# Pooled keys in pieces of 64, 16 and 64, and early sums and masks on TensorE, in a pooled and local attention with a feed-forward part

## The chip, the cores and the metric

The kernel runs on one core of a Trainium2 chip. The core has a matrix engine (TensorE, in the profile PE, with its weight loads as PEld), a vector engine (VectorE, DVE), a scalar engine (ScalarE, ACT), GpSimd (POOL), and SyncE (SP), which here only issues DMA transfers. TensorE reads SBUF, the working memory of 128 partitions, and writes PSUM, eight banks of 512 f32 values per partition. The metric is the device time of one execution in microseconds; it is a median over several runs.

## The reference

Inputs q, k and v are 8 batches x 8 heads x 576 tokens x 64 values. For each head two attentions are added. The result of all heads of a token, 512 values, goes through a feed-forward part with a softmax-weighted activation and a layer norm.

```python
# factor 4: means over four neighbouring tokens, 144 pooled tokens
q_d = q.reshape(B, H, Sd, 4, D).mean(axis=3)      # k_d, v_d the same way
out_d = sm_attn(q_d, k_d, v_d)                    # softmax(q k^T / 8) v
out_up = np.repeat(out_d, 4, axis=2)
# local: token i sees tokens j with |i - j| < 4
mask = np.abs(pos[:, None] - pos[None, :]) < 4
out_local = softmax(np.where(mask, scale * q @ k^T, -1e9)) @ v
x = (out_up + out_local) as 4608 tokens x 512
# feed-forward
h = x @ w_in                                      # 512 -> 1024, weights given as float64
solu = h * softmax(h)
ln = (solu - mean) / sqrt(var + 1e-6) * g_ln
return ln @ w_out                                 # 1024 -> 512
```

## The kernel before

**Steps and their order.** The kernel writes its work as a list of numbered steps (`plan`), and the string `ORDER` at its head gives the order in which they are issued: 2099 numbers before. Nothing reorders them afterwards; each engine, and SyncE's DMA queue, takes its instructions in that order and waits where one needs another engine. Steps 0 to 23 are `keep_clock`, pairs of matmuls on zeros that keep TensorE busy. The last loop of the function runs the plan.

**A batch.** For the first two batches (`EarlyBatch`) q and k of a head pair are loaded with six tokens per partition, turned by ordinary f32 matmuls with an identity (tiles `qp` and `kp`, L478) and copied to `qT` and `kT` (L484). For the other six, `Batch.pair_steps` loads 32x32 blocks and turns them on VectorE (L411, L415). In all eight, `sums` (L367) adds four neighbouring tokens of `qT` and `kT` on VectorE into `qd_flat` and `kd`; the division by 4 is left to a scale in the softmax.

**Local attention** (`Local.by_tensor`, five units a batch, each with two windows of 64 tokens for all heads): scores `sc` on TensorE (L614); on VectorE the mask is added while the scores leave PSUM (L632), and the maximum taken (L637); GpSimd subtracts it (L639); ScalarE takes the exponential (L641); VectorE sums (L644); GpSimd multiplies by the reciprocal (L650); TensorE turns the result (`plt`, L660), ScalarE copies it (L663), TensorE multiplies by v (`xp`, L670). A branch for a mask by TensorE is there (`early`), but `MASKED = 0` leaves it unused.

**Pooled attention** (`Pooled.steps`, one unit per head pair): the 144 pooled queries are taken in three chunks of 48 (`QC`, `QN`). Scores `sd` (L696) lie with 64 rows of one chunk and head in each half of the partitions. After the softmax (L703 to L720) `pdt` (L731) turns the weights with 12 transposes into two pieces of 72 keys on 72 partitions; two copies (L738, L741 or L743) bring them to `pdT`; `po` (L752) multiplies by the pooled v, `vd`, for two key pieces and two heads. `load_vs` loads v for the pooled sums in four transfers a batch, of 72 partitions each; GpSimd adds (L434, L437).

**Where matmuls sit in the array.** A matmul with at most 64 rows of input (partitions) and 64 columns of weights takes a quarter of the 128x128 array; the quarter follows from the partitions of its input and its output. `sc`, `xp` and `sd` are of this kind. `pdt` uses halves by rows, `po`, `qp` and `kp` halves by columns, and `plt` and the feed-forward matmuls the whole array.

**Weights and feed-forward.** w_in and w_out come as float64 in 16 pieces. ScalarE and VectorE make f32 of the two halves of each number (L323 to L338); ScalarE rounds to fp32r (L360), GpSimd takes the rest (L362), so that three products of rounded parts give the precision. For w_out, ScalarE first multiplies by `g_ln` (L358). A feed-forward tile has 128 tokens: `xhl` splits x (L919, L922), `ffn_in` makes h with 24 matmuls (L770) and the activation, `ffn_back` and `ffn_ut` bring it back turned through DRAM and VectorE (L866, L872, L874), `ffn_out` makes 24 matmuls (L888) and writes the output.

Of the kernel before, what the change touches and what calls it, by code (L numbers as in the profile page):

```python
# [129 lines left out]
def pooled_local_attention_then_solu_ffn(  # L130
# [701 lines left out]


    away = {}
    ON_PE = (NTILE - 1,)

    LATE = range(29, NTILE - 1)

# [203 lines left out]
```

## Time and profile before

| what | before |
|---|---|
| median of 3 runs | 601.65 us (601.19 to 605.02) |
| the profiled execution | 602.74 us, its span 601.0 us |
| granted TensorE clock, mean | 0.989 |
| busy: TensorE, VectorE, ScalarE, GpSimd | 574.8, 396.5, 361.8, 375.6 us |
| DMA | 94.34 MB, mean 157 GB/s |

The span reaches from the first to the last instruction of the program that was profiled; the execution's own time is 1.7 us longer. A line L752 is line 752 of the kernel. An f32 matmul shows as two records in the profile, a transpose as one. In rows of the timeline a block's length includes the time that its last matmul needs to run through the array, while the next block has begun already; so blocks are compared by the distance of their starts.

### The profile page before, as it was taken

What the parts mean: (1) busy time and instruction counts of PE and PEld (TensorE: products, weight loads), DVE (VectorE), ACT (ScalarE), POOL (GpSimd) and SP (SyncE); (2) the same over time, 40 slices, a digit from 0 to 9 for tenths busy, and PEclk for the clock granted to TensorE, in tenths of its full rate; (3) what the DMA queues carried; (4) which work ended last, traced back from release to release, by engine and by line L of the source; (5) the groups of instructions that cost most, each with busy time, mean ns of one, the idle gap of its engine ahead of it and who ended that gap; (6) DMA issues with size and microseconds to landing.
All of it is one profiled execution on the core that took longest, in us unless ns stands there. A gap on an engine that the chain in (4) does not pass through costs nothing.

```text
span 601.0 us, 15341 instructions
## 1 busy us (share of the span) xinstructions
PE 574.8 (96%) x5912; PEld 447.1 (74%) x5912; DVE 396.5 (66%) x692; ACT 361.8 (60%) x800; POOL 375.6 (62%) x553
## 2 busy tenths in 40 slices
PE   6889789899999999999999999999999999999996
PEld 3666557677777777787877777777777878788785
DVE  5989999869747677766856767737655533643541
ACT  3758866577745566566664854657465655553443
POOL 2576668867784778678574777656786767332221
PEclk8979999899999999999999999999999999999999
DMA  8999776687769767766878567847416623124230
GB/s 231 238 251 254 140 183 146 164 178 162 195 144 189 171 167 186 170 148 175 190 151 201 143 173 182 185 114 195 97 59 188 146 89 114 63 88 151 96 123 35
DMA packets 203913, 94.34 MB, mean 157 GB/s; under 512 B 162496, under 2 KB 192704, under 8 KB 203840
## 3 DMA queue, kind: packets, MB, share of 16 engines
q1 hardware_dynamic: 203840, 93.37, 63.3%
q8 instruction: 46, 0.75, 0.6%
q14 instruction: 27, 0.22, 0.1%
HBM read 65.54 MB, written 27.79 MB: 155 GB/s over the span
## 4 chain that ended last, share of the span: by engine, by line
PE 75%; POOL 6%; DVE 5%; ACT 4%; SPq 4%; DMA 3%; issue 3%; POOLq 0%; DVEq 0%
PE o L888 31%; PE h L770 27%; PE xp L670 3%; PE plt L660 3%; PE po L752 3%; PE sc L614 2%; DMA qm<-in_q_dram 2%; SPq L245 2%; PE pdt L731 2%; PE sd L696 2%; POOL pl L639 2%; DMA v<-u 1%; SPq L264 1%; POOL pd L720 1%; DVE w L334 1%
## 5 line engine op out<-in xcount | busy, mean ns | idle before, releaser
L888 PE MATMUL o<-wo_h,uh 128*128 128x512 f32 x288 | 117.9, 409 | 0.8 <-ACT uh L872 0.7
L770 PE MATMUL h<-wi_h,xh 128*128 128x512 f32 x288 | 116.3, 404 | 0.6 <-DVE e L785 0.6
L770 PE MATMUL h<-wi_h,xl 128*128 128x512 f32 x288 | 114.3, 397 | 1.3 <-POOL xl L922 1.3
L888 PE MATMUL o<-wo_l,uh 128*128 128x512 f32 x288 | 114.5, 398 | 0.0
L770 PE MATMUL h<-wi_l,xh 128*128 128x512 f32 x288 | 114.1, 396 | 0.0
L874 POOL TENSOR_TENSOR ul<-v,uh 128x512 fp32r<-128x512 f32 x58 | 74.4, 1288 | 19.7 <-ACT uh L872 7.7
L778 DVE TENSOR_REDUCE nmx<-h 128x1 f32<-128x1024 f32 x36 | 43.9, 1219 | 63.8 <-PE h L770 63.8
L888 PE MATMUL o<-wo_h,ul 128*128 128x512 f32 x288 | 79.1, 396 | 0.4 <-DVE ul L874 0.4
L782 ACT ACTIVATE e<-h,nmx 128x1024 f32<-128x1024 f32 x36 | 40.0, 1112 | 51.0 <-DVE nmx L778 51.0
L888 PEld LDWEIGHTS o<-wo_h,uh 128*128 128x128 f32 x288 | 54.6, 190 | 15.6 <-ACT uh L872 1.4
L770 PEld LDWEIGHTS h<-wi_h,xl 128*128 128x128 f32 x288 | 54.2, 188 | 15.2 <-POOL xl L922 2.1
L770 PEld LDWEIGHTS h<-wi_h,xh 128*128 128x128 f32 x288 | 54.2, 188 | 14.8 <-issue 1.0
L888 PEld LDWEIGHTS o<-wo_h,ul 128*128 128x128 f32 x288 | 54.2, 188 | 14.0 <-DVE ul L874 0.8
L770 PEld LDWEIGHTS h<-wi_l,xh 128*128 128x128 f32 x288 | 54.3, 189 | 12.2
L888 PEld LDWEIGHTS o<-wo_l,uh 128*128 128x128 f32 x288 | 54.5, 189 | 11.8
L922 POOL TENSOR_TENSOR xl<-x,xh 128x512 fp32r<-128x512 f32 (+1 forms) x40 | 47.1, 1183 | 18.6 <-ACT xh L919 17.4
L807 ACT ACTIVATE e<-e,nmu 128x1024 f32<-128x1024 f32 x35 | 40.1, 1146 | 28.2 <-POOL nmu L790 28.1
L785 DVE SCALAR_TENSOR_TENSOR e<-h,e 128x1024 f32<-128x1024 f32 x36 | 43.7, 1214 | 19.9 <-ACT e L782 19.9
L650 POOL TENSOR_TENSOR pl<-pl,rsl 128x512 f32<-128x512 f32 x40 | 42.1, 1055 | 20.7 <-DVE rsl L648 18.2
L866 DVE STREAM_TRANSPOSE v<-v 128x512 f32<-128x512 f32 x70 | 46.3, 688 | 12.5 <-DMA v<-u 12.5
L872 ACT ACTIVATE uh<-v 128x512 fp32r<-128x512 f32 x70 | 42.9, 623 | 14.9 <-DVE v L866 11.0
L639 POOL TENSOR_TENSOR pl<-pl,mxl 128x512 f32<-128x512 f32 x40 | 41.8, 1052 | 9.0 <-DVE mxl L637 4.6
(95 smaller groups left out, 1076.1 us busy)
## 6 DMA issues: line engine op xcount, KB each, us to landing
u<-e SPq DMA_DIRECT2D x35, 512.0 KB
v<-u SPq DMA_DIRECT2D x140, 128.0 KB
vw<-in_v_dram SPq DMA_DIRECT2D x160, 64.0 KB
vs<-in_v_dram SPq DMA_DIRECT2D x32, 288.0 KB
out_dram<-osb SPq DMA_DIRECT2D x36, 256.0 KB
qm<-in_q_dram SPq DMA_DIRECT2D x96, 72.0 KB
km<-in_k_dram SPq DMA_DIRECT2D x96, 72.0 KB
w<-in_moe_w_out_dram SPq DMA_DIRECT2D x8, 512.0 KB
```

The costliest lines, as they stand in the source:

```text
L639: nc.gpsimd.tensor_tensor(out=pl, in0=pl, in1=max_bc, op=ALU.subtract)
L650: nc.gpsimd.tensor_tensor(out=pl, in0=pl, in1=rs.unsqueeze(3).broadcast_to([P, NPR, 2, W]), op=ALU.mult)
L770: nc.tensor.matmul(hps[:, n, :], src[:, cc, :], wt[:, cc, n * 512:(n + 1) * 512], start=(cc == 0 and src is xh and wt is wi_h), stop=(cc = ...
L778: nc.vector.tensor_reduce(out=nmx, in_=hf, op=ALU.max, axis=AX.X, negate=True)
L782: nc.scalar.activation(e, hf, AF.Exp, bias=nmx, scale=1.0, accum_out=se)
L785: nc.vector.scalar_tensor_tensor(out=e, in0=hf, scalar=1.0, in1=e, op0=ALU.mult, op1=ALU.mult, accum_out=su)
L807: nc.scalar.activation(e, e, AF.Identity, bias=nmu, scale=1.0)
L866: nc.vector.transpose(vg, vg)
L872: nc.scalar.activation(uh, tp, AF.Copy)
L874: (nc.vector if v is None or i in LATE else nc.gpsimd).tensor_tensor(out=ul, in0=tp, in1=uh.bitcast(F32), op=ALU.subtract)
L888: nc.tensor.matmul(o, src[:, j, :], wt[:, 4 * g + j, :], start=(g == 0 and j == 0 and src is uh and wt is wo_h), stop=(g == 1 and j == 3 a ...
L922: nc.gpsimd.tensor_tensor(out=l, in0=src, in1=h.bitcast(F32), op=ALU.subtract)
```

## The change

- `KEYS`: the 144 pooled keys are taken in pieces of 64, 16 and 64 instead of 72 and 72. `vd` becomes a tile of 128 partitions with one head of a pair in each half; v is loaded in three pieces a batch with two transfers each, the 16-key piece always into one buffer, `few`; the other large buffers are five instead of six. `pdt` is 18 ordinary matmuls instead of 12 transposes, `pdT` is filled by one copy instead of two, and `po` has three pieces for each head. `sd` takes its chunks in the order 0, 2, 1.
- `MASKED = 2`: for batches 0 and 1 the mask goes into `sc` by two bf16 matmuls ahead of the scores; VectorE takes the maximum from PSUM and subtracts it while the scores leave PSUM.
- `SUM_PE = 2`: for batches 0 and 1 the sums over four tokens are matmuls with the identity, added up in PSUM, and two copies.
- `G_LATE`: `g_ln` is multiplied in while the high half of w_out is rounded, and again on VectorE while the low half is taken.
- `OTHER`: 135 numbered steps run on another engine than usual, most of them on VectorE instead of GpSimd or ScalarE (the helper `engine`).
- `keep_clock` takes a new tile each time, and its 24 steps stand elsewhere in the order.
- A new `ORDER` of 2041 steps. It begins with loads of q and k; the old one began with pieces of w_in. A masked local unit has one step less, a pooled unit one, a batch's values two.

```diff
+    KEYS = ((0, 64), (64, SD - 128), (SD - 64, 64))
+    ORDER_C = (0, 2, 1)
-    MASKED = 0
+    MASKED = 2
+    SUM_PE = 2
+    G_LATE = True
...
+    other = {int(n) for n in OTHER.split()}
+    def engine(usual, instead):
+        return instead if now[0] in other else usual
...
+    def load_vs(b, c):
+        (p0, n), name = KEYS[c], f"vs_{b}_{c}"
+        vs = (big(name) if n == 64 else few).rearrange("p (r x) -> p r x", r=NPR)
+        for par in range(2):
+            nc.sync.dma_start(
+                vs[rows(par)][0:n],
+                v[b, par::2, FAC * p0:FAC * (p0 + n), :].rearrange("h (p t) d -> p h (t d)", t=FAC),
+            )
...
+                if G_LATE:
+                    nc.scalar.activation(hi, t, AF.Copy, scale=g)
+                    yield
+                    nc.vector.scalar_tensor_tensor(
+                        out=lo, in0=t, scalar=g, in1=hi.bitcast(F32), op0=ALU.mult, op1=ALU.subtract
+                    )
...
+            sp = ps_t.tile([P, 2, SD], F32, tag="t", name=f"qs_{self.b}_{pr}")
+            for n, src in enumerate((self.qT, self.kT)):
+                by_four = src[:, pr].rearrange("x (s f) -> x s f", f=FAC)
+                for f in range(FAC):
+                    nc.tensor.matmul(
+                        sp[:, n], ident, by_four[:, :, f], start=f == 0, stop=f == FAC - 1
+                    )
+            yield
+            for n, dst in enumerate((self.qd[pr], self.kd[:, pr])):
+                copy(engine(nc.scalar, nc.vector), dst, sp[:, n])
...
-            for c in (0, 1, 2):
-                for par in (0, 1) if c != 1 else (1, 0):
+            for c in ORDER_C:
+                for par in (0, 1):
                     nc.tensor.matmul(
-                        sd[rows((par + c) % 2), (0, 2, 1)[c], :],
+                        sd[rows(par ^ (c == 2)), c, :],
...
-            for kc in range(2):
-                for j in range(QC):
-                    for x in range(2):
-                        c = (2 * j + x) % QC
-                        nc.tensor.transpose(
-                            pt[:, x, kc, j, :], pd[rows(x), (0, 2, 1)[c], kc * 72:(kc + 1) * 72],
-                            ident[rows(x), rows(x)],
+            for kc, (k0, _) in enumerate(KEYS):
+                for c in ORDER_C:
+                    for par in (0, 1):
+                        src = rows(par ^ (c == 2))
+                        nc.tensor.matmul(
+                            pt[rows(par), c, kc, :],
+                            pd[src][0:QN, c, k0:k0 + 64],
+                            ident[src][0:QN, src][:, 0:QN], start=True, stop=True,
                         )
...
-            for kc in range(2):
+            for kc, (_, n) in enumerate(KEYS):
                 for par in range(2):
...
+                    at = rows(par)
+                    nc.tensor.matmul(
+                        po[at, :], bt.vd[at][0:n, kc, pr, :], pdT[at][0:n, kc, :],
+                        start=kc == 0, stop=kc == len(KEYS) - 1,
+                    )
```

More of the change, by code (lines that the diff above doesn't have):

```diff
@@ L26 @@
 ORDER = """
[99 rows of a table removed]
[96 rows of a table added]
+"""
+OTHER = """
[7 rows of a table added]
 """
@@ L219, in pooled_local_attention_then_solu_ffn, with copy @@
         nc.vector.memset(pl, 1e-9)
+    few = cpool.tile([P, 1024], F32, name="few")
+    nc.gpsimd.memset(few, 0.0)
     qd_flat = cpool.tile([P, NPR * SD + 64 - QN], F32, name="qd_flat")
     nc.vector.memset(qd_flat[:, NPR * SD:], 0.0)
+    other = {int(n) for n in OTHER.split()}
+    now = [None]
+    def engine(usual, instead):
+        return instead if now[0] in other else usual
+    def copy(eng, out, in_):
+        if eng is nc.scalar:
+            nc.scalar.activation(out, in_, AF.Copy)
+        else:
+            eng.tensor_copy(out=out, in_=in_)
     def two_banks(pool, tag, name):
@@ L233, in small_bank @@
     def small_bank(b, n):
-        return (ps_o, "o") if b < 2 and n % 2 and not W_PSUM and not WARM else (ps_t, "t")
+        return (ps_o, "o") if b < 2 and n % 2 and not WARM else (ps_t, "t")
     def load_q_k(t, b, pr):
@@ L270, in big @@
     def big(name):
-        return load.tile([P, 1024], F32, tag="big", name=name, bufs=6)
-    def load_vs(b, c, hs):
-        vs = big(f"vs_{b}_{c}_{hs.start}")[0:72].rearrange("p (h x) -> p h x", h=H // 2)
-        nc.sync.dma_start(
-            vs, v[b, hs, c * 288:(c + 1) * 288, :].rearrange("h (p t) d -> p h (t d)", t=FAC)
-        )
+        return load.tile([P, 1024], F32, tag="big", name=name, bufs=5)
+    def load_vs(b, c):
[6 more added lines that the diff above has]
+            )
         return vs
@@ L324, in f32 @@
             yield
-            nc.vector.tensor_scalar(
+            engine(nc.vector, nc.gpsimd).tensor_scalar(
                 out=t, in0=t, scalar1=F64_LO, scalar2=F64_HI, op0=ALU.max, op1=ALU.min
@@ L357, in piece @@
                 fc = n - 2 * NCC
-                nc.scalar.activation(t, t, AF.Copy, scale=self.g[:, fc:fc + 1])
+                g = self.g[:, fc:fc + 1]
                 hi, lo = wo_h[:, fc, :], wo_l[:, fc, :]
+                if G_LATE:
[5 more added lines that the diff above has]
+                    yield
+                    return
+                nc.scalar.activation(t, t, AF.Copy, scale=g)
             nc.scalar.activation(hi, t, AF.Copy)
             yield
-            nc.gpsimd.tensor_tensor(out=lo, in0=t, in1=hi.bitcast(F32), op=ALU.subtract)
+            engine(nc.gpsimd, nc.vector).tensor_tensor(
+                out=lo, in0=t, in1=hi.bitcast(F32), op=ALU.subtract
+            )
             yield
@@ L424, in out, with pooled_vload, pooled_vsum @@
             return xs[self.b]
-        def value(self, kc, head):
-            return [self.vd[:, kc, head, :]]
-        def pooled_vload(self, c, hs):
-            self.vs[c, hs.start] = load_vs(self.b, c, hs)
-        def pooled_vsum(self, c, hs):
-            vs = self.vs.pop((c, hs.start))
-            nc.gpsimd.tensor_tensor(
+        def pooled_vload(self, c):
+            self.vs[c] = load_vs(self.b, c)
+        def pooled_vsum(self, c):
+            vs = self.vs.pop(c)
+            eng = engine(nc.gpsimd, nc.vector)
+            eng.tensor_tensor(
                 out=vs[:, :, 0:2 * D], in0=vs[:, :, 0:2 * D], in1=vs[:, :, 2 * D:4 * D], op=ALU.add
             )
-            nc.gpsimd.tensor_tensor(
-                out=self.vd[:, c, hs], in0=vs[:, :, 0:D], in1=vs[:, :, D:2 * D], op=ALU.add
+            eng.tensor_tensor(
+                out=self.vd[:, c], in0=vs[:, :, 0:D], in1=vs[:, :, D:2 * D], op=ALU.add
             )
@@ L483, in pair_steps @@
                 yield
-                nc.scalar.activation(
+                copy(
+                    engine(nc.scalar, nc.vector),
                     dst.rearrange("x (p a t) -> x p a t", a=2, t=HT),
-                    tp[:, :, 0:n].rearrange("x a (t p) -> x p a t", t=HT), AF.Copy
+                    tp[:, :, 0:n].rearrange("x a (t p) -> x p a t", t=HT),
                 )
                 yield
-            sums(self.qd[pr], self.qT[:, pr])
+            if self.b >= SUM_PE:
+                sums(self.qd[pr], self.qT[:, pr])
+                yield
+                sums(self.kd[:, pr], self.kT[:, pr])
+                yield
+                return
+            sp = ps_t.tile([P, 2, SD], F32, tag="t", name=f"qs_{self.b}_{pr}")
[5 more added lines that the diff above has]
+                    )
             yield
-            sums(self.kd[:, pr], self.kT[:, pr])
+            for n, dst in enumerate((self.qd[pr], self.kd[:, pr])):
+                copy(engine(nc.scalar, nc.vector), dst, sp[:, n])
             yield
@@ L495, in accumulate @@
         if first:
-            nc.scalar.activation(x, part, AF.Copy)
+            copy(engine(nc.scalar, nc.vector), x, part)
         else:
@@ L616, in by_tensor @@
                         bt.qT[rows(par), pr, s0:s0 + W], bt.kT[rows(par), pr, s0:s0 + W],
-                        start=not early, stop=True,
+                        start=not early, stop=not early or pr == NPR - 1,
                     )
@@ L638, in by_tensor @@
                 yield
-                nc.gpsimd.tensor_tensor(out=pl, in0=pl, in1=max_bc, op=ALU.subtract)
+                engine(nc.gpsimd, nc.vector).tensor_tensor(
+                    out=pl, in0=pl, in1=max_bc, op=ALU.subtract
+                )
                 yield
@@ L649, in by_tensor @@
             yield
-            nc.gpsimd.tensor_tensor(
+            engine(nc.gpsimd, nc.vector).tensor_tensor(
                 out=pl, in0=pl, in1=rs.unsqueeze(3).broadcast_to([P, NPR, 2, W]), op=ALU.mult
@@ L662, in by_tensor @@
             plT = wk.tile([P, NPR, 2, W], F32, tag="plT", name=f"plT_{b}_{u}")
-            nc.scalar.activation(plT, pt, AF.Copy)
+            copy(engine(nc.scalar, nc.vector), plT, pt)
             yield
@@ L719, in steps @@
             yield
-            nc.gpsimd.tensor_tensor(
+            engine(nc.gpsimd, nc.vector).tensor_tensor(
                 out=pd, in0=pd, in1=rs.unsqueeze(2).broadcast_to([P, QC, SD]), op=ALU.mult
@@ L735, in steps @@
[L735 to L736 removed]
+            pt = two_banks(ps_a, "a", f"pdt_{b}_{pr}").rearrange("p a n -> p (a n)")
+            pt = pt[:, 0:QC * 256].rearrange("p (j n) -> p j n", n=256)
+            pt = pt[:, :, 0:len(KEYS) * QN].rearrange("p j (k n) -> p j k n", n=QN)
+            for kc, (k0, _) in enumerate(KEYS):
[6 more added lines that the diff above has]
+                            ident[src][0:QN, src][:, 0:QN], start=True, stop=True,
+                        )
@@ L737, in steps @@
+            pdT = wk.tile([P, len(KEYS), QC, QN], F32, tag="pdT", name=f"pdT_{b}_{pr}")
             yield
-            nc.scalar.activation(pdT[:, :, :, 0, :], pt[:, 0], AF.Copy)
+            copy(
+                engine(nc.scalar, nc.vector) if b < 2 else engine(nc.vector, nc.scalar),
+                pdT.rearrange("p k j n -> p j k n"), pt,
+            )
             yield
-            if b < 2:
-                nc.scalar.activation(pdT[:, :, :, 1, :], pt[:, 1], AF.Copy)
-            else:
-                nc.vector.tensor_copy(out=pdT[:, :, :, 1, :], in_=pt[:, 1])
@@ L744, in steps @@
-            yield
-            pdT = pdT.rearrange("p k j x n -> p k (j x n)")
+            pdT = pdT.rearrange("p k j n -> p k (j n)")
             pool, tag = small_bank(b, pr)
             po = pool.tile([P, SD], F32, tag=tag, name=f"po_{b}_{pr}")
-            for kc in range(2):
+            for kc, (_, n) in enumerate(KEYS):
                 for par in range(2):
-                    parts = bt.value(kc, 2 * pr + par)
-                    for n, vt in enumerate(parts):
-                        nc.tensor.matmul(
-                            po[par * 64:par * 64 + 64, :], vt, pdT[:, kc, par * SD:(par + 1) * SD],
-                            start=(kc == 0 and n == 0), stop=(kc == 1 and n == len(parts) - 1),
-                        )
+                    at = rows(par)
+                    nc.tensor.matmul(
+                        po[at, :], bt.vd[at][0:n, kc, pr, :], pdT[at][0:n, kc, :],
+                        start=kc == 0, stop=kc == len(KEYS) - 1,
+                    )
@@ L806, in ffn_in @@
         else:
-            nc.scalar.activation(e, e, AF.Identity, bias=nmu, scale=1.0)
+            if engine(nc.scalar, nc.vector) is nc.scalar:
+                nc.scalar.activation(e, e, AF.Identity, bias=nmu, scale=1.0)
+            else:
+                nc.vector.tensor_scalar(
+                    out=e, in0=e, scalar1=1.0, scalar2=nmu, op0=ALU.mult, op1=ALU.add
+                )
         s = small.tile([P, 1], F32, tag="s", name=f"s_{i}", bufs=6)
@@ L921, in xhl @@
         for src, h, l in parts:
-            nc.gpsimd.tensor_tensor(out=l, in0=src, in1=h.bitcast(F32), op=ALU.subtract)
+            engine(nc.gpsimd, nc.vector).tensor_tensor(out=l, in0=src, in1=h.bitcast(F32), op=ALU.subtract)
         splits[i] = xh, xl
@@ L940, in pooled_local_attention_then_solu_ffn @@
     weights = Weights()
-    idle = []
     def keep_clock(n):
-        if not idle:
-            idle.append(ps_o.tile([P, 512], F32, tag="o", name="warm"))
+        o = ps_o.tile([P, 512], F32, tag="o", name=f"warm_{n}")
         for _ in range(2):
             nc.tensor.matmul(
-                idle[0].rearrange("p (a n) -> p a n", n=P), zeros,
+                o.rearrange("p (a n) -> p a n", n=P), zeros,
                 zeros.unsqueeze(1).broadcast_to([P, 4, P]), start=True, stop=True,
@@ L975, in values @@
     def values(bt):
-        for m in range(4):
-            hs = slice(m // 2 * 4, m // 2 * 4 + 4)
-            step(bt.pooled_vload, m % 2, hs)
-            step(bt.pooled_vsum, m % 2, hs)
+        for c in range(len(KEYS)):
+            step(bt.pooled_vload, c)
+            step(bt.pooled_vsum, c)
     def attention(bt):
+        late = bt.b == 0
+        local = [Local(bt, u, not late) for u in range(5)]
+        pooled = [Pooled(bt, pr, late) for pr in range(NPR)]
         values(bt)
-        local = [Local(bt, u, bt.b > 0) for u in range(5)]
-        pooled = [Pooled(bt, pr, bt.b == 0) for pr in range(NPR)]
-        for it in pooled + local if bt.b == 0 else local + pooled:
+        for it in pooled + local if late else local + pooled:
             if isinstance(it, Local):
                 step(bt.load_v, it.u)
-            row(it.steps(), 10 if isinstance(it, Pooled) or bt.b < MASKED else 11)
+            row(it.steps(), 9 if isinstance(it, Pooled) else 11 - (bt.b < MASKED))
     tiles = 0
@@ L1007, in pooled_local_attention_then_solu_ffn @@
     for n in ORDER.split():
-        fn, args = plan[int(n)]
+        now[0] = int(n)
+        fn, args = plan[now[0]]
         fn(*args)
```

14 lines of the change are left out of this document (6 added, 8 removed), and 202 rows, old and new, of tables (ORDER, OTHER).

## The prediction

> **What bounds the kernel now.** I read the page first: busy shares, the 40 slices, then the chain that ended last.
>
> ```profile
> span 601.0 us, 15341 instructions
> PE 574.8 (96%) x5912; PEld 447.1 (74%) x5912; DVE 396.5 (66%) x692; ACT 361.8 (60%) x800; POOL 375.6 (62%) x553
> ...
> DVE  5989999869747677766856767737655533643541
> PEclk8979999899999999999999999999999999999999
> ...
> PE 75%; POOL 6%; DVE 5%; ACT 4%; SPq 4%; DMA 3%; issue 3%; POOLq 0%; DVEq 0%
> ```
>
> TensorE is busy 96% of the span and is three quarters of the chain. VectorE is near full only in the first quarter. So I cut the run into five stretches: until the first q arrives, until the first feed-forward tile (62.9), until the first scores of batch 2 (115), until the last output matmul, and the end. Columns: length, then busy time and count for PE, PEld, DVE, ACT, POOL, granted clock, DMA share, GB/s.
>
> ```profile
> 0.00:10.60 10.60, 5.58 (x14) 1.89 (x14) 5.01 (x13) 2.90 (x4) 1.72 (x11) 1.00 0.82 213
> 10.60:62.90 52.30, 45.29 (x848) 34.47 (x848) 47.08 (x82) 38.20 (x103) 31.91 (x30) 0.90 1.01 243
> 62.90:115.00 52.10, 44.28 (x548) 33.46 (x542) 50.09 (x83) 36.61 (x74) 39.07 (x44) 0.97 0.70 159
> 115.00:596.90 481.90, 479.46 (x4513) 377.31 (x4512) 294.33 (x516) 283.45 (x620) 302.86 (x470) 1.00 0.59 147
> 596.90:601.00 4.10, 0.15 (x1) 0.00 (x0) 0.00 (x0) 0.69 (x1) 0.00 (x0) 1.00 0.17 64
> ```
>
> From 115 on TensorE is idle 2.4 us of 481.9, at full clock: there the time is the sum of TensorE's work, and no other engine's work counts. All slack lies before 115: 7.0 us idle in the second stretch, 7.8 in the third, and the 10.6 before the first q. VectorE is 90% and 96% busy in the two middle stretches, and the DMA engines are full in the first of them. So the question has two parts: how TensorE's sum after 115 changes, and how much TensorE work added before 115 fits into about 15 us of gaps.
>
> **What a TensorE block costs.** The timeline shows which blocks are longer than their matmuls. Columns: start, length, instruction, count.
>
> ```profile
> 122.97 0.71 PE L752 MATMUL po<-pdT,vd 72*64 72x144 f32 x8
> 123.61 1.20 PE L696 MATMUL sd<-kd,qd_flat 64*64 64x144 f32 x24
> 124.74 0.71 PE L752 MATMUL po<-pdT,vd 72*64 72x144 f32 x8
> ...
> 169.64 1.16 PE L614 MATMUL sc<-kT,qT 64*64 64x64 f32 x64
> 170.73 0.66 PE L660 MATMUL plt<-ident,pl 128*128 128x128 f32 x4
> 171.32 0.69 PE L670 MATMUL xp<-plT,vw 64*64 64x58 f32 x32
> 171.94 0.50 PE L770 MATMUL h<-wi_h,xh 128*128 128x512 f32 x1
> ...
> 177.75 0.53 PE L731 MATMUL pdt<-ident,pd 64*72 64x64 f32 x12
> 178.21 0.71 PE L752 MATMUL po<-pdT,vd 72*64 72x144 f32 x8
> 178.85 0.69 PE L670 MATMUL xp<-plT,vw 64*64 64x56 f32 x32
> 179.47 0.50 PE L888 MATMUL o<-wo_h,uh 128*128 128x512 f32 x1
> ```
>
> I go by start to start. 64 records of sc take 1.09, 32 of xp (the same 64x64 tiling) 0.62: 32 more cost 0.47, so coming in from another tiling costs 0.62 - 0.47 = 0.15 us. The two sd blocks in a row take 1.13 = 2 x 0.49 + 0.15; po takes 0.64 = 0.49 + 0.15; pdt takes 0.46 = 0.31 + 0.15. Now count records per part of the array. sc puts 8 of its 32 on each quarter: 0.47 / 8 = 58 ns. sd puts 4, 4, 2, 2 of its 12 on the quarters, po 4 and 4 on two column halves: both give 0.49 / 4 = 122 ns for 144 columns. pdt puts 6 and 6 on two row halves: 52 ns. So a block lasts as long as its fullest part: records there times 122 ns (144 columns) or 58 ns (64). xp takes the same 0.62 with 56 columns as with 58 (0.62 at 171.32), so I let 48 columns cost 58 ns too.
>
> **The pooled pieces.** How many records an instruction makes:
>
> ```profile
> L752 PE MATMUL po<-pdT,vd 72*64 72x144 f32 x256 | 23.2, 303 | 0.0
> L731 PE MATMUL pdt<-ident,pd 64*72 64x64 f32 x384 | 16.5, 221 | 2.1 <-POOL wi_l L362 1.3 <-ACT kT L484 0.5 <-ACT pd L711 0.3
> L478 PE MATMUL qp<-ident,qm 96*64 96x96 f32 x192 | 11.3, 277 | 4.7 <-DMA qm<-in_q_dram 2.8 <-ACT pdT L741 1.6 <-DVE x L498 0.3
> ```
>
> The 32 blocks of pdt have 12 transposes each and 384 records: one each. The 8 blocks of qp have 12 ordinary f32 matmuls and 192 records: two each. The change turns 12 transposes into 18 ordinary matmuls, so 36 records; per piece of keys, query chunks 0 and 1 use the diagonal quarters and chunk 2 the other two, so a diagonal quarter gets 12 records: 12 x 58 ns = 0.70 us, against 0.31: +0.39. po goes from 4 to 6 matmuls; head 0 uses the first diagonal quarter for all three pieces, head 1 the other, so 6 records each: 0.73 against 0.49: +0.24. The 16-key piece streams 144 columns like the others. Against this, sc, xp, sd, pdt and po now share one tiling. Going through the two printed orders block by block, I count 215 changes of tiling before and 182 after; from the first scores of batch 2 on, 160 and 105. That leaves 26 pdt and 28 po blocks after that point: 26 x 0.39 + 28 x 0.24 - 55 x 0.15 = 10.1 + 6.7 - 8.2 = **+8.6 us** where TensorE has no gap. Bounds: with all records spread evenly over four quarters (9 x 58 ns, 3 x 122 ns) it is 5.5 - 3.4 - 8.2 = -6.1; with a tiling of its own for the 16-row piece (no row shows fewer than 64 rows) two more changes in each po block add 28 x 2 x 0.15 = 8.4. I take +8.6: po's rows already show each part of the array working through its own records one after another, with nothing shared out.
>
> [...]
>
> **Sums and mask on TensorE.** Per head pair 2 x 4 matmuls of 144 columns, 16 records on the whole array: 16 x 122 ns = 1.95, eight times 15.6 us. Below, plt's 4 records in 170.73 to 171.32 less 0.15 give 110 ns (14.1 us); above, if reading every fourth element halves the rate, 31. The row nearest in columns is po's, so 15.6. The mask is 20 matmuls of 256 columns; half of the warm row's mean of 325 ns, cold starts in it, is 0.16 at most, so 2 to 3 us, taken as 2.3.
>
> ```profile
> L947 PE MATMUL warm<-zeros 128*128 128x512 bf16 x48 | 15.6, 469 | 2.3 <-POOL zeros L211 2.3
> L367 DVE TENSOR_REDUCE kd<-kT 128x144 f32<-128x576 f32 x32 | 23.4, 738 | 0.8 <-ACT kT L484 0.6
> L367 DVE TENSOR_REDUCE qd_flat<-qT 128x144 f32<-128x576 f32 x32 | 23.3, 735 | 0.7 <-ACT qT L484 0.7
> L325 DVE TENSOR_SCALAR w<-w 128x512 f32<-128x512 f32 x16 | 12.9, 814 | 5.6 <-ACT w L323 5.6
> L632 DVE TENSOR_TENSOR pl<-sc,mask 128x512 f32<-128x512 f32 x40 | 26.7, 675 | 12.8 <-PE sc L614 12.7
> L874 DVE TENSOR_TENSOR ul<-v,uh 128x512 fp32r<-128x512 f32 x12 | 9.0, 765 | 7.6 <-ACT uh L872 5.5 <-issue 2.1
> ```
>
> VectorE loses 16 sums (16 x 0.737 = 11.8) and 4 clamps that the list OTHER gives to GpSimd (3.3). In masked units its mask add (0.675) becomes a subtract of the same shape: nothing. It gains the low halves of w_out (8 x 0.765) and of five w_in pieces (3.8), and from OTHER before that point five q/k copies, three pairs of sum copies and three single steps (by L632, about 7): 17 against 15. So VectorE, near full before 115, is not relieved. GpSimd and ScalarE are (one split and the masked subtracts, a scaling and a pdT copy), but neither was late for long there.
>
> **The first 115 us.** TensorE's added work up to the first scores of batch 2: sums 15.6, mask 2.3, 6 pdt x 0.39 = 2.3, 4 po x 0.24 = 1.0, 22 more changes of tiling x 0.15 = 3.3: 24.5 us. The warm-up pairs stay 24. What takes it up:
>
> ```profile
> 0.72 0.39 SPq L314 DMA_DIRECT2D w<-in_moe_w_in_dram  x1
> 2.10 0.45 SPq L463 DMA_DIRECT2D qm<-in_q_dram  x1
> 10.63 2.19 PE L478 MATMUL qp<-ident,qm 96*64 96x96 f32 x24 [2.78 <-DMA qm<-in_q_dram]
> ```
>
> Two weight pieces and one k, 1.34 MB, are issued ahead of the first q; the new order issues q first. At the first stretch's 213 GB/s that is about 6 us sooner. Then come the 7.0 + 7.8 of gaps, and the clock of 0.90 and 0.97, worth 5.2 + 1.6 if a denser TensorE kept it full. If everything fills, the stage grows by 24.5 - 6 - 14.8 - 6.8 = -3 (I bound it at 0, since VectorE's sum is the same); if only the start helps, +18.5. I take half of gaps and clock: 24.5 - 6 - 7.4 - 3.4 = **+8 us**.
>
> Hidden at no cost behind TensorE after 115: OTHER's moves from GpSimd and ScalarE to VectorE (some hundred steps of 0.6 to 0.8, about 60 us; 294 + 60 of 482 is still no bound), the single pdT copy, three pooled v pieces for four, two more SP issues a batch, the single buffer for the 16-key piece (used once a batch; behind its load wait other loads on SP), five big buffers for six. If that cover failed, each late step would show as a TensorE gap of about its own 0.7 us.
>
> **Sum.** Profiled execution 602.74 (span 601.0) + 8.6 + 8 = 619.3; the median lies 1.1 lower: **618 us**.
>
> **Rivals.**
> - *Quarters fill evenly* (not slower): if blocks of one tiling flow into each other, so that idle quarters take the neighbour's records, the late stage gives -6.1 and the early one about 2.5 less work: 602.7 - 6.1 + 5.5 - 1.1 = 601, 594 with all gaps filled. It decides when a po block takes no more than its old 0.49. For it: the two sd blocks cost no change between them. Against: pdt and po load the diagonal most, and so does sd next to them.
> - *The 16-row piece is its own tiling*: 618 + 8.4 = 626. [...]
> - *Added on top*: gaps before 115 are waits that stay, since VectorE and the loads are as full: 602.7 + 18.5 + 8.6 - 1.1 = 629.
> - *Hidden anyway*: DMA sets the first 63 us, and all early work disappears in it: 602.7 + 0 + 8.6 - 1.1 = 610, 606 if the late stage gains more per change.
>
> **How the numbers follow.** Forecast (612 to 624) 0.45, own tiling 0.18, on top 0.10, hidden 0.15, even quarters 0.12. A difference of 1% is 6 us, about what a measurement tells. Faster by over 1% needs the even quarters and full gaps: 0.04. Within 1% (595.6 to 607.7): rest of that rival and the low end of the hidden case: 0.12. Slower: 0.84. The range runs from 604 to 631, the on-top case with its margin.
>
> **What would show it.** Right: pdt blocks of about 0.70 and po of 0.73 where no tiling changes; 36 and 12 records each; sums of about 2 us a pair; TensorE still without gaps after the first scores of batch 2, which come at about 123; a TensorE sum after that point longer by 8 to 9 us. Wrong: po at 0.5 or less, or the first scores of batch 2 before 115.

## The result and the profile after

| | before | after |
|---|---|---|
| median, measured side by side | 602.33 us (601.19 to 605.02, 4 runs) | 642.75 us (641.51 to 643.90, 4 runs) |
| the profiled execution; its span | 602.74; 601.0 | 642.08; 639.7 |
| first q block; first feed-forward matmul | 10.6; 62.9 | 4.3; 86.2 |
| first scores of batch 2; from there to the start of the last output matmul | 115.0; 481.7 | 137.3; 498.0 |

The change makes the kernel 6.6% slower (ratio 1.066, interval 1.062 to 1.071). Of the 38.7 us by which the span grew, 22.3 lie before the first scores of batch 2 and 16.3 behind them. The forecast was 618 with a range to 631, with +8 and +8.6 in the two places. Each run below has the median of its fast executions as its time, which leaves out one execution of 1127.98 us in b_keys_po64 and one of 1434.21 us in a_no_sums_own.

The head of the page after, its rows for VectorE and the clock, and the two lines of the chain that ended last:

```profile
span 639.7 us, 17342 instructions
...
PE 625.9 (98%) x6956; PEld 485.2 (76%) x6956; DVE 473.5 (74%) x796; ACT 331.9 (52%) x741; POOL 278.5 (44%) x445
...
DVE  5567689998887789868888799856977767544541
...
PEclk9999998999999999999999999999999999999999
...
PE 79%; DVE 10%; issue 3%; POOL 3%; SPq 1%; ACT 1%; DMA 1%; POOLq 0%; DVEq 0%; ACTq 0%
PE o L950 26%; PE h L826 25%; PE qs L542 5%; PE po L808 4%; PE pdt L790 3%; PE xp L728 3%; PE sc L670 3%; PE plt L718 3%; PE sd L754 2%; PE qp L520 2%; PE warm L1007 2%; PE kp L520 1%; POOL ul L936 1%; DVE nmx L834 1%; DMA v<-u 1%
```

TensorE has 51 us more work (574.8 before) and the chain names a new line, qs (L542, the sums), with 5%. VectorE's busy time rose by 77 us and GpSimd's fell by 97, as OTHER's moves have it. The same stretches as before, cut at the marks of the table (length, busy time and count of PE, PEld, DVE, ACT and POOL, clock, DMA share, GB/s):

```profile
4.30:86.20 81.90, 81.84 (x1135) 61.20 (x1135) 51.95 (x95) 39.36 (x106) 21.95 (x20) 1.00 0.83 193
86.20:137.30 51.10, 46.87 (x605) 35.02 (x607) 49.78 (x78) 30.93 (x63) 32.68 (x34) 0.97 0.61 144
137.30:635.60 498.30, 495.12 (x5229) 388.58 (x5220) 369.37 (x616) 259.68 (x571) 221.27 (x380) 1.00 0.55 141
```

Up to the first feed-forward matmul TensorE is now busy 81.84 of 81.90 us, at a granted clock of 1.00 (45.3 of 52.3 and a clock of 0.90 before); the loads, which had the DMA engines at 1.01 there, now have them at 0.83. The second stretch has VectorE busy 49.8 of 51.1. In the last one TensorE is idle 3.2 us of 498.3. Two blocks of the timeline show what grew (start, length, instruction, count):

```profile
10.84 2.21 PE L542 MATMUL qs<-qT,ident 128*128 128x144 f32 x8
12.87 2.23 PE L542 MATMUL qs<-kT,ident 128*128 128x144 f32 x8
14.92 0.61 PE L1007 MATMUL warm<-zeros 128*128 128x512 bf16 x2
...
213.81 1.60 PE L790 MATMUL pdt<-ident,pd 48*64 48x48 f32 x72
215.24 1.21 PE L808 MATMUL po<-pdT,vd 64*64 64x144 f32 x12
216.38 0.50 PE L950 MATMUL o<-wo_h,uh 128*128 128x512 f32 x1
```

Start to start, eight records of a sum take 12.87 - 10.84 = 2.03 us: 254 ns each where 122 was forecast, so 4.1 us a pair. Two pdt blocks take 1.43, and po begins 0.05 after the start of their last record: 0.72 each, where 0.70 was forecast. po takes 1.14; forecast were 0.73 for its records and 0.15 for the change to the tiling of the next block, `o`: 0.88.

### The profile page after: what moved, and what is told of

Its sections match the earlier page's. It is cut to its first block, busy times and chain, and to the rows that moved or that the text cites. A ratio compares the mean times of both kernels' runs of the same rounds, so it can differ in the third digit from the quotient of the medians.

```text
span 639.7 us, 17342 instructions
## 1 busy us (share of the span) xinstructions
PE 625.9 (98%) x6956; PEld 485.2 (76%) x6956; DVE 473.5 (74%) x796; ACT 331.9 (52%) x741; POOL 278.5 (44%) x445
## 4 chain that ended last, share of the span: by engine, by line
PE 79%; DVE 10%; issue 3%; POOL 3%; SPq 1%; ACT 1%; DMA 1%; POOLq 0%; DVEq 0%; ACTq 0%
PE o L950 26%; PE h L826 25%; PE qs L542 5%; PE po L808 4%; PE pdt L790 3%; PE xp L728 3%; PE sc L670 3%; PE plt L718 3%; PE sd L754 2%; PE qp L520 2%; PE warm L1007 2%; PE kp L520 1%; POOL ul L936 1%; DVE nmx L834 1%; DMA v<-u 1%
## 5 line engine op out<-in xcount | busy, mean ns | idle before, releaser
L950 PEld LDWEIGHTS o<-wo_h,ul 128*128 128x128 f32 x288 | 53.8, 187 | 14.6 <-POOL ul L936 1.4
L950 PEld LDWEIGHTS o<-wo_l,uh 128*128 128x128 f32 x288 | 54.1, 188 | 13.1 <-DVE wo_l L396 1.6
L936 POOL TENSOR_TENSOR ul<-v,uh 128x512 fp32r<-128x512 f32 x32 | 42.4, 1326 | 45.5 <-ACT uh L933 34.1
L957 ACT ACTIVATE osb<-o,s 128x512 f32<-128x512 f32 x36 | 24.5, 680 | 37.6 <-PE o L950 25.9
L864 ACT ACTIVATE e<-e,nmu 128x1024 f32<-128x1024 f32 x27 | 30.9, 1147 | 24.9 <-POOL nmu L846 24.9
L695 POOL TENSOR_TENSOR pl<-pl,mxl 128x512 f32<-128x512 f32 x24 | 25.4, 1064 | 40.8 <-DVE mxl L693 34.0
L936 DVE TENSOR_TENSOR ul<-v,uh 128x512 fp32r<-128x512 f32 x38 | 30.1, 809 | 17.5 <-ACT uh L933 17.5
```

Source lines behind the costliest of these rows:

```text
L695: engine(nc.gpsimd, nc.vector).tensor_tensor(out=pl, in0=pl, in1=max_bc, op=ALU.subtract)
L864: nc.scalar.activation(e, e, AF.Identity, bias=nmu, scale=1.0)
L936: (usual if v is None else engine(usual, nc.vector)).tensor_tensor(out=ul, in0=tp, in1=uh.bitcast(F32), op=ALU.subtract)
L950: nc.tensor.matmul(o, src[:, j, :], wt[:, 4 * g + j, :], start=(g == 0 and j == 0 and src is uh and wt is wo_h), stop=(g == 1 and j == 3 a ...
```

## The experiments

My theory from these rows: TensorE's own sum is still the time, and two of its terms were sized wrong, the read with a step of four elements (early) and the 16-key piece (late). Its rivals: the rate belongs to the whole-array f32 matmul and not to the step; VectorE or the loads set the early stage; the new order, not the pieces, carries the late part. The table gives each run's time, its ratio to the kernel before on the same chip, the first feed-forward matmul, the first scores of batch 2 and the late stage (from those scores to the start of the last output matmul), in us. Single executions of a run lie 1 to 7 us apart, so a difference of 1 or 2 us between two medians says little.

| run | time | ratio | first h | batch 2 | late |
|---|---|---|---|---|---|
| a_sums_contig | 629.94 | 1.044 (1.040 to 1.049) | 73.1 | 124.1 | 498.0 |
| a_sums_by2 | 628.93 | 1.044 (1.039 to 1.049) | 73.7 | 124.8 | 498.1 |
| a_pick_po64 | 629.46 | 1.043 (1.039 to 1.047) | 81.4 | 132.5 | 491.6 |
| a_po64 | 633.59 | 1.049 (1.044 to 1.054) | 85.5 | 136.6 | 491.5 |
| a_contig_po64 | 621.00 | 1.029 (1.026 to 1.032) | 70.3 | 121.4 | 490.5 |
| b_keys | 631.65 | 1.048 (1.043 to 1.052) | 68.8 | 122.9 | 501.9 |
| b_keys_po64 | 620.77 | 1.030 (1.026 to 1.033) | 69.3 | 123.4 | 491.2 |
| b_sums | 638.14 | 1.056 (1.050 to 1.062) | 94.2 | 146.3 | 481.1 |
| a_no_sums | 639.54 | 1.058 (1.052 to 1.063) | 80.8 | 135.3 | 498.0 |
| a_no_sums_own | 637.60 | 1.057 (1.053 to 1.061) | 77.3 | 131.8 | 498.3 |
| a_no_sums_warm | 638.10 | 1.058 (1.055 to 1.061) | 80.6 | 134.5 | 497.8 |
| a_po64_half | 630.54 | 1.045 (1.042 to 1.049) | 80.0 | 133.8 | 491.2 |
| a_order_only | 647.78 | 1.073 (1.068 to 1.078) | 79.1 | 141.7 | 497.9 |

### What the sums cost

**Read in a row.**

```diff
- sp[:, n], ident, by_four[:, :, f], ...
+ sp[:, n], ident, src[:, pr, f * SD:(f + 1) * SD], ...
```

> The changed kernel, in which the sums' matmuls read 144 columns in a row instead of every fourth one (they then add the wrong tokens; batches 0 and 1 are not the reference's). Stride theory (reading every fourth element halves the rate): a record falls from 254 to about 125 ns, a pair from 4.1 to about 2.1 us, the time to 624 to 631. Rival (the rate is that of a 128-row f32 matmul that accumulates, whatever it reads): 254 ns and 640 to 645.

The blocks in its timeline, and its first two stretches:

```profile
11.64 1.14 PE L542 MATMUL qs<-qT,ident 128*128 128x144 f32 x8
12.62 1.14 PE L542 MATMUL qs<-kT,ident 128*128 128x144 f32 x8
13.60 0.59 PE L1007 MATMUL warm<-zeros 128*128 128x512 bf16 x2
```
```profile
4.30:73.10 68.80, 67.37 (x1136) 53.04 (x1135) 52.40 (x95) 39.33 (x106) 22.60 (x20) 0.98 0.92 226
73.10:124.10 51.00, 46.78 (x603) 34.94 (x603) 49.69 (x78) 30.91 (x63) 32.63 (x34) 0.97 0.63 145
```

Eight records take 0.98 us: 122.5 ns each, the forecast's figure to the nanosecond. Instruction, weights, columns and accumulation are the same, only the step differs, so the rival falls. The run is 12.8 us faster, of which 13.1 come out of the first stretch; the second keeps its 51 us.

**Which step does it.**

```diff
- by_four = src[:, pr].rearrange("x (s f) -> x s f", f=FAC)   # read: by_four[:, :, f]
+ by_two = src[:, pr].rearrange("x (s f) -> x s f", f=2)      # read: by_two[:, f // 2 * SD:][:, 0:SD, f % 2]
```

> The changed kernel, in which the sums' matmuls read every second column instead of every fourth (they then add the wrong tokens of batches 0 and 1): a step of 8 bytes where the change has 16. Theory that any step costs the rate: a record stays at 254 ns, 8 records at 2.03 us, the time at 640 to 645. [...]

```profile
12.94 1.18 PE L542 MATMUL qs<-qT,ident 128*128 128x144 f32 x8
13.96 1.18 PE L542 MATMUL qs<-kT,ident 128*128 128x144 f32 x8
14.98 0.59 PE L1007 MATMUL warm<-zeros 128*128 128x512 bf16 x2
```

1.02 us for eight records, 127 ns each: against the 122.5 ns of the read in a row a step of 8 bytes costs 4%, one of 16 bytes 107%. The theory that any step costs the rate falls: the run takes 628.93 us where that theory had 640 to 645. Why a step of 16 bytes halves the rate and one of 8 hardly touches it isn't shown; the runs have no other step.

**A sum that reads in a row and adds the right tokens.** `pick` holds ones where one of a row's tokens belongs to the column's four.

```diff
- sp[:, n], ident, by_four[:, :, f], start=f == 0, stop=f == FAC - 1
+ sp[rows(par), n], self.qk[nm, pr][:, par, t], pick[:, t // 2], start=t == 0, stop=t == self.TT - 1
```

> The changed kernel with po's 16-key piece over 64 rows and the sums on TensorE in another way that reads in a row: the weights are the untransposed q and k (96 rows by 64 columns, as in the transposes), the moving operand a 0/1 matrix of 144 columns that picks the four tokens, six matmuls a head added up. Per pair 48 records in two column halves, 24 x 122 ns = 2.9 us instead of 4.1. Stride theory: 8 x 1.2 = 9.4 us less than 633.6: 622 to 627. Rival (the sums cost by their 144 columns and their accumulation whatever they read): 2 x 24 records at 254 ns, 6.1 us a pair, 645 to 652.

```profile
13.05 1.69 PE L551 MATMUL qs<-pick,qm 96*64 96x144 f32 x24
14.57 1.64 PE L551 MATMUL qs<-pick,km 96*64 96x144 f32 x24
16.14 0.60 PE L1017 MATMUL warm<-zeros 128*128 128x512 bf16 x2
```
```profile
4.80:81.40 76.60, 74.90 (x1392) 60.94 (x1391) 53.28 (x95) 39.11 (x106) 23.10 (x24) 0.98 0.84 197
```

1.52 us for 12 records in each column half is 127 ns a record, as the stride theory says. A pair takes 3.09 instead of 4.08, 7.9 us over eight pairs, but the run is only 4.1 us faster than a_po64: the first q block came 0.5 us later, and from there to the first feed-forward matmul 76.6 us pass where a_po64 has 81.2, so 4.6 of the 7.9 come out. In the row above TensorE is idle 1.7 us of that stretch and its clock is 0.98, where a_po64 is busy 75.64 of its first 75.70 us at 1.00; 0.02 of 76.6 us are another 1.5, which accounts for the rest.

### The 16-key piece

```diff
- po[at, :], bt.vd[at][0:n, kc, pr, :], pdT[at][0:n, kc, :],
+ po[at, :], bt.vd[at][:, kc, pr, :], pdT[at][:, kc, :],
```

> The changed kernel with po's matmul of the 16-key piece taken over all 64 rows (rows 16 to 63 of the summed v are zero, so the result is the same). Theory that the 16-row piece is a tiling of its own: two changes less in each of 32 po blocks, a block from 1.14 to 0.87 us start to start, 32 x 0.27 = 8.6: 632 to 636. Rival (the pieces wait for each other's accumulation, or the block's 12 records simply cost 1.14): 640 to 645.

The same place of its timeline, and its late stretch:

```profile
211.92 1.60 PE L790 MATMUL pdt<-ident,pd 48*64 48x48 f32 x72
213.35 0.92 PE L808 MATMUL po<-pdT,vd 64*64 64x144 f32 x12
214.20 0.50 PE L950 MATMUL o<-wo_h,uh 128*128 128x512 f32 x1
```
```profile
136.60:628.20 491.60, 487.41 (x5228) 391.92 (x5219) 368.88 (x616) 259.92 (x571) 221.80 (x380) 1.00 0.56 143
```

po falls from 1.14 to 0.85 with the same 12 records: 0.29, about the 2 x 0.15 at which two changes of tiling were priced. The starts of single records show where it lies. In the kernel before, the last three of the four pairs of po's records (one for each head) in the block at 122.97 start 0.12 us apart. In the kernel after the six pairs start at 215.24, 215.38, 215.60, 215.77, 215.99 and 216.16: from the first 16-row pair, the third, and again from the first pair that has 64 rows once more, a step of 0.22 and one of 0.17 stand where the kernel before has steps of 0.12, together 0.29 more. The late stage is 6.5 us shorter, the profiled span 7.3, the median 9.2. Here the block with its 16 keys over 64 rows, 48 of them zero, is cheaper than the one with them over 16: 0.85 against 1.14.

**Both terms out.** The edits of a_sums_contig and a_po64 together.

> The changed kernel with both suspected terms taken out: the sums' matmuls read 144 columns in a row (they then add the wrong tokens) and po's 16-key piece runs over 64 rows. If the two terms are separate and both on TensorE's path, as their single runs say (12.8 and 9.2 us off 642.75), they add up: 618 to 624, the first scores of batch 2 at 122 to 125, the late stage 490 to 493. If another engine takes over when TensorE gets both (VectorE, busy 102 of 120 us up to there): 625 to 632.

```profile
4.30:70.30 66.00, 64.12 (x1135) 51.76 (x1135) 53.21 (x95) 39.34 (x106) 22.37 (x20) 1.00 0.95 231
70.30:121.40 51.10, 45.34 (x608) 33.89 (x608) 49.78 (x79) 30.95 (x63) 32.69 (x34) 1.00 0.68 155
121.40:612.10 490.70, 486.88 (x5228) 391.56 (x5220) 368.91 (x616) 259.92 (x571) 221.74 (x380) 1.00 0.56 143
```

21.75 us off, 12.8 + 9.2 = 22.0 were expected: within the spread of the executions (618.77 to 621.68) the terms add up. This kernel, in which both of the forecast's prices hold, takes 621.0; the forecast was 618.

### The parts in the old order

**The pieces alone**, with the 16-key piece over 16 rows and then over 64. Both take the new `load_vs`, `vd`, `sd`, `pdt` and `po` into the kernel before:

```diff
- for m in range(4): ...                       # 8 steps, four tiles of v
+ for cs in ((0,), (1, 2), (), ()): ...        # 8 steps, three pieces of v
- two pdT copies, a step each
+ one pdT copy, an empty step
```

> The kernel before with the pieces of 64, 16 and 64 alone (old order, sums and mask on VectorE; the three loads and sums of v fall in the first two of the four old steps, the one pdT copy in the first of the two; five big buffers). TensorE theory: 28 late blocks x (0.39 + 0.24 + 2 x 0.135) = +25, changes of tiling counted in the old order 160 against 163 with the 16-row piece as its own: 482 to about 500 in the late stage (its po's own two changes are in that count), total 619 to 626. Rival (the pieces are cheap and the new order carries the late 16 us): 602 to 610.

> The kernel before with the three pieces, po's 16-key piece over all 64 rows. TensorE theory: 28 x 0.63 = 17.6 of records, 53 changes of tiling fewer in the late stage (107 against 160) x 0.15 = 8.0: +9.7 late, 1 to 3 early: 611 to 616, about 9 us under the pieces alone. Rival (quarters fill evenly, or the tiling changes are worth nothing): the same time as the pieces alone, or under 605.

Their late stretches:

```profile
122.90:624.90 502.00, 497.16 (x5249) 390.00 (x5248) 298.12 (x516) 275.18 (x594) 287.13 (x454) 1.00 0.56 141
```
```profile
123.40:614.80 491.40, 487.72 (x5249) 391.68 (x5248) 298.38 (x516) 275.09 (x594) 286.67 (x453) 1.00 0.57 144
```

Late, the pieces cost +20.2 and, over 64 rows, +9.5 (forecast for the latter: +9.7). The old order with the pieces over 64 rows needs 491.2, the new order (a_po64) 491.5: late, the order and OTHER's moves together are worth nothing, though VectorE is busy 298 us in the one and 369 in the other. The rival that the order carries the late part falls. Both runs came out 5 to 6 us above what was expected of them: early the pieces cost +8, about twice what the six pdt and four po blocks there explain. The granted clock in the two early stretches was lower too (0.88 and 0.91 in b_keys, 0.83 and 0.94 in b_keys_po64, 0.90 and 0.97 before), and the five buffers and the two loads in one step may share in it; I didn't separate these.

**The sums alone**, in the second of the two old steps. Here too `keep_clock` takes a new tile each time, since the sums use its bank:

```diff
- sums(self.qd[pr], self.qT[:, pr]); yield; sums(self.kd[:, pr], self.kT[:, pr]); yield
+ yield; (the eight matmuls of the change, two copies on ScalarE); yield
```

> The kernel before with the sums of batches 0 and 1 on TensorE alone (old order; matmuls and copies in the second of the two old steps, in the bank of the warm-up). They add 8 x 4.1 + about 1 = 34 us to TensorE before the first scores of batch 2, where it had 15 us of gaps and a clock of 0.90 and 0.97, and take 11.8 from VectorE. TensorE theory: +15 to +30, that point at 130 to 145, total 617 to 633. Rival (VectorE and the loads set this stage in the kernel before, the gaps take the sums): 598 to 610.

```profile
10.80:94.20 83.40, 77.47 (x977) 58.00 (x977) 38.20 (x69) 41.66 (x118) 31.65 (x30) 0.98 0.74 171
94.20:146.30 52.10, 45.58 (x538) 34.23 (x538) 48.35 (x78) 36.62 (x74) 39.09 (x44) 0.93 0.54 130
```

The first scores of batch 2 come 31.3 us later for some 34 us of added TensorE work: in the old order the gaps take up little (TensorE's idle time in the two stretches falls from 7.0 and 7.8 us to 5.9 and 6.5), although VectorE lost its sums. The new order places the same matmuls so that its first stretch, starting 6 us earlier, ends at 86.2 instead of 94.2.

### What else holds the early stage

**No sums on TensorE**, with `SUM_PE = 0`, order and OTHER as changed.

> The changed kernel with the sums over four tokens of batches 0 and 1 back on VectorE; order and everything else as changed. TensorE theory (TensorE alone sets the early stage): 8 x 4.1 = 32.5 us of TensorE work go, VectorE gains 16 x 0.74 = 11.8 in a stretch where it was busy 52 of 82 us: 610 to 621, the first scores of batch 2 at 105 to 116 instead of 137. Rival (VectorE or the loads set the early stage, TensorE only follows them): 636 to 655.

This is where my theory failed. 32.5 us of TensorE work go and the run gains 3.2, with the first scores of batch 2 at 135.3 where 105 to 116 were expected:

```profile
4.30:80.80 76.50, 61.81 (x1008) 42.80 (x1007) 59.54 (x101) 36.45 (x94) 21.98 (x19) 0.80 0.90 209
80.80:135.30 54.50, 48.05 (x605) 35.59 (x606) 52.74 (x82) 31.85 (x64) 33.06 (x34) 0.94 0.56 133
```

No engine is full in the first stretch. The chain of waits goes from one to the next (start, length, what):

```profile
29.73 9.43 DMA qm<-in_q_dram
...
45.03 6.61 DMA w<-in_moe_w_out_dram
51.65 2.32 DMA vw<-in_v_dram
53.98 0.75 DVE qT L254
54.73 0.66 DVE qd_flat L411
...
62.98 1.22 PE sd L754 x12
64.20 1.41 PE pdt L790 x36
65.61 1.85 PE po L808 x12
67.47 2.12 PE qp L520 x24
```

It runs over late loads, then over a row of VectorE steps with the sums among them, then over TensorE blocks that take up to twice their time (qp 2.12, against 1.14 for most qp blocks of the kernel after): the granted clock is 0.80 over the whole stretch. In the kernel before, the qp block at 10.63 took the same 2.12 us from start to start, and the granted clock there, from 10.6 to 13.9 us, was 0.50. Three runs asked which of these matters.

**Moves of the early steps undone:** `OTHER` only from step 636 on.

> The changed kernel with the sums back on VectorE (as in the run that took only 3 us off) and, for the steps of batches 0 and 1 with their tiles and weights, no moves between engines: some 15 steps (low halves of w_in, q, k, pdT and x copies) leave VectorE before the first scores of batch 2, four clamps come back to it. VectorE theory (with the sums on it, VectorE sets the early stage, busy 112 of 131 us): about 7 to 9 us less work there, 630 to 635 against 639.5. Rival (the order and the loads set it, whoever does the steps): 637 to 643.

**More warm-up:** four matmuls instead of two in each `keep_clock`.

> The changed kernel with the sums back on VectorE and the 24 warm-up pairs on TensorE doubled to four matmuls each (about 10 us more TensorE work, results unused). In the run without the doubling TensorE's clock was 0.80 up to 81 us, a q transpose block took 2.12 us instead of 1.14. Clock theory (the gaps left by the sums cost the clock, and slow TensorE blocks then lie on the path): clock over 0.9 and 629 to 636. Rival (VectorE alone sets that stage): 638 to 646.

**Half the sums:** `SUM_PE = 1`, with po over 64 rows.

> The changed kernel with po's 16-key piece over 64 rows, and the sums on TensorE for batch 0 alone, those of batch 1 on VectorE. TensorE loses 4 x 4.1 = 16.4 us up to the first scores of batch 2, VectorE gains 8 x 0.74 = 5.9. Two-limits theory (with all sums TensorE sets that stage at 137, with none VectorE at 135, so between them lies a lower point): 620 to 628 against 633.6. Rival (VectorE or the order keep it at 135 as soon as any sum leaves TensorE): 631 to 635.

The first two are 1.9 and 1.4 us faster than a_no_sums, whose executions lie between 634.38 and 640.34, so no gain is shown for either; both times lie in their rivals' ranges. The moved steps alone are not the cause. The doubled warm-up brought the clock of the first stretch to 0.86 only, so what a full clock would give stays open. The third gains 3.1 against a_po64, just outside the rival's span and far from the 6 to 13 that two separate limits would have given. What all runs share is the second stretch, from the first feed-forward matmul to the first scores of batch 2: in the new order 51.0 to 51.1 us wherever TensorE does all the sums, with VectorE busy 49.7 to 49.8 of them, and 53.8 to 54.5 in the runs above, where sums of batch 1 or of both stay on VectorE (52.5 to 53.1 busy). In the kernel after, the chain of waits through that stretch runs over VectorE steps and issue time (in which the engine waits for nothing that the profile shows), with under 2 us on TensorE and ScalarE. That stretch is VectorE's in these runs. The first stretch is TensorE's own sum in the kernel after, where it is idle 0.06 us; with both terms out (a_contig_po64) it is idle 1.9 us of 66.0 there, beside DMA engines at 0.95. With the sums on VectorE it is a chain through loads, VectorE and a slowed TensorE, and which of them would have to change first isn't settled.

**Order alone:** sums, mask and pieces as before, in the new order. The mask step of batches 0 and 1 writes earlier than the new order allows for, so scores of an earlier unit can be lost there.

> The changed kernel with three of its four parts undone: the keys in two pieces of 72 with transposes again (four loads and sums of v in three steps, two pdT copies in one step), sums and mask of batches 0 and 1 on VectorE; the new order, the list of moved steps and g at w_out's rounding stay. TensorE theory: the late stage is before's 482 less some changes of tiling, the early stage starts 6 us sooner: 594 to 604. Rival (the new order itself costs, through VectorE, the moved steps or late loads): 610 to 625.

At 647.78 us it lies outside both ranges, and it doesn't answer its question. Four loads and sums of v in three steps put sums in a row on GpSimd (three of them on the chain, from 108 to 114 us), and TensorE waits in the late stage too, idle 14.6 of 498.2 us. Two of the longest of these waits (what waited, for what; us in total, times, longest):

```profile
PE o L947 <- DVE ul L933: 3.9, 1, 3.9
PE h L823 <- DVE e L838: 1.9, 3, 0.8
```

What causes the late waits isn't shown. That its late stage is as long as that of the kernel after says nothing for the order: TensorE is busy 483.6 us of it here, 495.1 there. The old-order runs stand in its place. None of the runs beats the kernel before.

## Why the prediction was right or wrong

**TensorE's sum is the late stage: right.** 3.2 us idle after the first scores of batch 2, in the kernel before 2.4.

**Cost of a block by its fullest part: right.** Single records show the parts: in the kernel before, the 64x64 records of sc start four at a time, each four 58 ns after the last; those of po (72x64) and pdt (64x72) two at a time, 122 and 56 ns apart; those of plt (128x128) one at a time, 109 ns apart. pdt 0.72 (forecast 0.70), po over 64 rows 0.85 (forecast 0.73 and one change of 0.15), 36 and 12 records. With the pieces over 64 rows in the old order the late stage grew by 9.5 us: records of 28 x 0.63 and 53 changes fewer, forecast +9.7. The rival of evenly filled quarters is out.

**"sc, xp, sd, pdt and po now share one tiling": wrong.** This is the failed step of the late part. With the 16-key piece over 16 rows po takes 0.29 us more than over 64, as if it left the shared tiling for that piece and came back; that a matmul with at most 64 rows takes a quarter of the array, as said ahead of the prediction, doesn't give this price. Counted again with two more changes in a block, the late stage has 161 changes of tiling, not 105, against 160 before: 10.1 + 6.7 + 0.2 = 17.0, and 16.3 was measured. The prediction named this case as a rival with nearly the right price (8.4 late; over 64 rows TensorE is busy 7.7 us less there, of which 6.5 came out as time) and gave it 0.18, because no row showed fewer than 64 rows. The 0.29 us lie where the records change from 64 rows to 16 and back, and are gone in a_po64; what else the array does at such a change, no run shows.

**Sums at 122 ns a record: wrong.** This is the failed term of the early part: 254 ns, 8 x 4.1 = 32.5 us instead of 15.6. The upper bound named the cause and almost the size (31). I took the row nearest in columns; that row reads its columns in a row, and the step was the one thing it couldn't price.

**The early stage, "+8": near with the forecast's price, in part by luck.** With the sums at the forecast rate (a_sums_contig) the first scores of batch 2 come at 124.1 (forecast 123). The start came 6.3 us earlier (forecast 6), TensorE's idle time in the two stretches fell by 9.2 us, from 14.8 to 5.6 (forecast 7.4), and the fuller clock was worth 3.9 (forecast 3.4), an estimate from 0.90 and 0.97 in the kernel before against 0.98 and 0.97. But half of the gaps was a choice that no row supported. The picture behind it, added TensorE work less what the gaps take up, holds only while the sums are on TensorE: without them that point comes at 135.3. "VectorE is not relieved" held, 104.2 us busy up to there against 102.2. What the forecast lacked is that VectorE sets the second stretch, so that its gaps on TensorE were not free to be filled: 4.2 us of 7.8 are still there in the kernel after.

**The range.** Each of the two unknowns had its upper end in the text. Both ends together give 618 + 15.4 + 8.4 = 641.8, and 642.75 was measured. That it is so close is in part luck: the two places gave 14.3 and 7.7 more than forecast. The range, to 631, held the second alone (626.4), the first not quite (633.4), and never both.

## What to carry to other kernels

Price a matmul's operand by its access pattern, not only by its shape: in this kernel a moving f32 operand read at every fourth element took twice as long as one read in a row or at every second (254 ns against 122.5 and 127). In a sequence of matmuls over 64 rows, try a short piece filled up with zero rows: here 64 rows were cheaper than 16, 0.85 us a block against 1.14. Where two unknown prices come from rows that don't show the operation, add their upper ends before drawing the range.

## What the runs showed of the hardware

- A 128x144 f32 record on the whole array: 122.5 ns read in a row, 127 ns at a step of 8 bytes, 254 ns at a step of 16.
- A po block with its 16-key piece over 16 rows took 0.29 us more than with it over 64 (1.14 against 0.85). That is more than the 0.24 at which I estimate the piece's own records, two in a row at 122 ns each.
- With the 32.5 us of sums off TensorE its granted clock in the first stretch was 0.80 instead of 1.00, and a qp block there took 2.12 us instead of 1.14.
